# Matmuls of zeros on TensorE ahead of, and in the early pauses of, a fused attention and MoE kernel

## The chip, the cores and the metric

The kernel runs on one core of one Trainium2 chip. The metric is the device time in microseconds of one execution, and the number for a kernel is the median of its runs. The engines are PE (TensorE matmuls, with PEld for its weight loads), DVE (VectorE), ACT (ScalarE), POOL (GpSimd) and SP (SyncE, which issues the loads and stores).

## The reference

The input is q, k and v with 8 batches, 8 heads, 576 positions and 64 dimensions. For each batch and head there are two attentions, which are added; the sum goes through a two-layer network with a leaky ReLU.

```python
q_d = q.reshape(B, H, Sd, factor, D).mean(axis=3)      # factor 4, Sd 144; k_d and v_d likewise
out_d = sm_attn(q_d, k_d, v_d)                         # softmax attention over the 144 pooled positions
out_up = np.repeat(out_d, factor, axis=2)
mask = np.abs(pos[:, None] - pos[None, :]) < factor    # local attention: 7 neighbours
scores = np.where(mask, scale * np.matmul(q, k.transpose(0, 1, 3, 2)), -1000000000.0)
...
out_local = np.matmul(attn, v)
x = (out_up + out_local), transposed and reshaped to 4608 x 512
h = x @ w_in                                           # 512 x 2048
g = np.maximum(0.01 * h, h)
return g @ w_out                                       # 2048 x 512
```

## The kernel before

**The order of the work** is written by a planner at build time. Every piece of work is a Python generator that asks for slots (buffers) and for operations on an engine, and yields the estimated duration of each. The class `Order` keeps a time for each engine and always takes the operation that can start first; between equal ones the lower rank (the first argument of `od.spawn`) goes first. Instructions are emitted in the order in which the planner takes them, so each engine's queue has a fixed order, and on the chip an instruction that isn't ready holds up all that stand behind it on its engine. In the planner an operation is done `HOP` = 0.2 us after its end.

**The network.** Columns of x are handled in chunks: chunk 0 has 512 columns and chunks 1 to 11 hold the rest. `up_proj` (L843) multiplies by w_in into the bank `hp`; `leaky` (L854 to L857) makes the two halves `gh` and `gl` of the activations on ACT and DVE; `down_proj` (L881) multiplies by w_out into the banks `acc0` to `acc3`. Each product is three matmuls of high and low parts. The weights come in blocks, `convert` loads one (L245) and unpacks it on ACT (L313), DVE (L315), ACT or DVE again (L326, L323) and POOL (L328); the buffer is free for the next load after L328.

**The first batch's attention** is done ahead of that, with four pairs of heads c = 0 to 3, from buffers whose names begin with `su_`. Two kinds of work are interleaved:

- `pooled(0, c)`: sums of four positions (DVE L428 for c = 0, POOL L422 and L424 for the others), the scores into the bank `acc{c}` (PE L444), the softmax (DVE L452 and L453, ACT L456, DVE L459 and L460, POOL L464), two transposes (PE L477, copied out by ACT L479), the values (PE L501, copied out by ACT L507). `vsums` sums v on DVE (L391) as its loads land.
- `banded(0, c, hf)`: the local attention's scores in two parts hf (PE L556 and L564), the softmax (DVE L571 and L572, ACT L575, DVE L577, ACT L579, DVE L581, POOL L583), transposes (PE L591, copied out by ACT L593), the values (PE L606), the sum with the pooled part (DVE L617) and the split into x (ACT L629, DVE L631).

After that, POOL and DVE compute the local attention of the other seven batches (L691, L697, L752, L758) beside PE's network.

**What the change touches.** `heads` are two tiles of 128x512 int32 that DVE clears at the start (L284); `convert` writes the upper half of each of their elements at L313, from 23 us on. `slot("acc3")` is one bank of PSUM; its first use is the pooled scores of c = 3. The planner's time of an operation on PE starts at the later of the time of PE and of what it waits for.

Of the kernel before, what the change touches and what calls it, by code (L numbers as in the profile page):

```python
# [10 lines left out]
BF16 = mybir.dt.bfloat16  # L11
# [14 lines left out]
NF, NE, NC = DF // 128, DM // 128, DM // 128  # L26
# [11 lines left out]
LSPLIT = 14  # L38
HALFS = 4
HF1 = 21  # L40


def plan():
# [161 lines left out]
def attn_moe(ctx: ExitStack, tc, qkt, vd, qb, kb, vb, vwb, band, identb, w_in, w_out, ident, edge, out):  # L205
    nc = tc.nc
# [12 lines left out]
    od = Order(bufs)  # L219

    def slot(*tags):
        return (yield ("slot", tags, 0))
# [6 lines left out]
    def bank(s):  # L229
        return ps.tile([128, 512], F32, name=s.tag, tag=s.tag, bufs=bufs[s.tag])  # L230

    def op(eng, n, *after, times=1, lock=False):
        if eng == "PE":
            dur = n
        else:
            a, k = COST[eng]
            dur = times * a + k * n
        return (yield ("op", eng, dur, max((0.0,) + after), 0, after, lock))
# [9 lines left out]
    def wait(name, n=1):  # L248
        return (yield ("wait", name, n))
# [3 lines left out]
    def fixed():  # L253
        yield from wait(("asked", 0, 0))
        for dst, src, name, size in ((idb_sb, identb, "idb", 32e3), (band_sb, band, "band", 160e3),
                                     (id_sb, ident, "id", 64e3)):
            od.signal(name, (yield from load(dst, src, size)))

    def edges():
        yield from wait("late")  # L260
        od.signal("edge", (yield from load(edge_sb, edge, 32e3)))
# [20 lines left out]
    heads = [axp.tile([128, DM], I32, name=f"head{i}") for i in range(bufs["head"])]  # L282
# [5 lines left out]
    def cleared():  # L288
        yield from wait(("x", 0, 0), NC)
        for t in qblks:  # L290
            nc.gpsimd.memset(t[:, :384], 0)
            od.signal("cleared", (yield from op("POOL", 200, 0.0)))

    stage = []

    def staging():
        s_x = yield from slot("x1")
        stage.append(sb(s_x, [128, bufs["stage"], HALFS * DM], U16))
        od.signal("stage")
        s_x.free((yield from wait("converted", 2 * NF)))  # L300
# [36 lines left out]
    def outd_tile(b):  # L337
        s = yield from slot("outd")
        outd[b] = sb(s, [128, NC, SD], F32)
        od.signal(("outd", b), s.t)  # L340
        t = yield from wait(("read", b), 8 if b < BANDED else 2 * len(PARTS[b]))
        s.free(t)

    def x_tile(i):
        if i > 1:
            yield from wait(("xbuf", i - 1))
        elif i:
            yield from wait("stage")
        s_x = yield from slot(f"x{i % 2}")
        both = sb(s_x, [128, 2, NC, XMAX[i % 2]], F32R)[:, :, :, :CHUNKS[i][1]]  # L350
        xt[i] = both[:, 0], both[:, 1]
        od.signal(("xbuf", i), s_x.t)
        s_x.free((yield from wait(("done", i), 2 if i == 0 else 1)))
        if i >= LAST - 2:
            od.signal(("over", i))
# [14 lines left out]
    def given(c):  # L370
        if c:
            yield from wait(("asked", 0, c - 1))
        kept[0, c] = sup.tile([128, 2, S], F32, name=f"qk{c}")
        tq = yield from load(kept[0, c], qkt[0, c], 590e3)
        od.signal(("asked", 0, c))
        od.signal(("qk", 0, c), tq)
# [139 lines left out]
    def windows(c, hf, pool):  # L516
        b0, b1 = BLKS[hf]
        if hf:
            yield from wait(("vd", 0, c))
        s_vw = yield from slot("su_vs" if hf else "su_vw")  # L520
        vws[c, hf] = s_vw, sb(s_vw, [WIN, b1 - b0, 2, D], F32, pool)
        t = yield from load(vws[c, hf][1][:, :b1 - b0], vwb[0, c, :, b0:b1], 35840 * (b1 - b0), s_vw.t)
        od.signal(("vw", c, hf), t)
# [401 lines left out]
    def make_room():  # L925
        for c in range(NC):
            yield from wait(("pooled", B - 1, c))
        yield from wait("converted", 2 * NF)
        t = yield from wait("values", len(ORD))
        ax.__exit__(None, None, None)  # L930
        fin[1] = ctx.enter_context(tc.tile_pool(name="fin1", bufs=1))
        for h in range(2):
            raw[1, h] = unit(1, f"r1{h}", [128, 2, EN], F32)
        xt[LAST] = [unit(1, f"b{h}", [128, 2, EN], F32R) for h in "hl"]
        od.signal(("xbuf", LAST), t)
        t = yield from wait("landed", len(ORD))
        at.__exit__(None, None, None)
        fin[2] = ctx.enter_context(tc.tile_pool(name="fin2", bufs=1, side="right"))
        od.signal("cleared2", t)
# [11 lines left out]
    def combine_x():  # L951
        t = yield from wait(("xbuf", LAST))
        s_s = yield from slot("sw1")
        for h in range(2):
            raw[0, h] = unit(1, f"r0{h}", [128, 2, EN], F32)
        tx = yield from wait(("x", LAST - 1, 0), LANDED[LAST - 1, 0])
        xh, xl = (x.bitcast(F32) for x in xt[LAST - 1])
        for h in range(2):
            t = yield from op("POOL", 2 * EN, t, tx)
            both("POOL", raw[0, h], xh[:, 2 * h:2 * h + 2], xl[:, 2 * h:2 * h + 2], ALU.add)  # L960
        od.spawn(-3.5, split_x24())
        od.spawn(-3.4, split_x31())
        T["B22"] = xt[LAST][::-1]
        od.signal("B22", (yield from wait(("x", LAST, 0), LANDED[LAST, 0] // 2)))
        for j, h in (("B11", 0), ("B21", 1)):
            T[j] = [x[:, 2 * h:2 * h + 2] for x in xt[LAST - 1][::-1]]
            od.signal(j, tx)
        tr = yield from wait("raw", LANDED[LAST, 0])
        for o, a, b, alu in (((1, 0), (1, 1), (1, 0), ALU.subtract), ((0, 0), (0, 0), (1, 0), ALU.add),
                             ((0, 1), (0, 1), (0, 0), ALU.subtract), ((1, 1), (1, 1), (0, 0), ALU.subtract)):  # L970
            t = yield from op("DVE", 2 * EN, t, tr, lock=True)
            both("DVE", raw[o], raw[a], raw[b], alu)
            od.signal(("T", o), t)
        od.signal("Tdone", t)
        s_s.free((yield from wait("x24")))
# [147 lines left out]
    def split():  # L1123
        for f in range(NF):
            t = yield from wait(("kept", f))
            t = max(t, (yield from wait("turned")))
            s_g, s_l = (yield from slot("gh")), (yield from slot("gl"))
            od.spawn(-9 + 0.1 * f, halved(f, G[f // 2][:, f % 2], s_g, s_l, t))
# [24 lines left out]
    with tc.manual_schedule():  # L1153
        od.spawn(0, fixed())
        od.spawn(30, cleared())
        for b in range(B):
            od.spawn(0, outd_tile(b))
        od.spawn(0, staging())
        for i in range(LAST):
            od.spawn(0, x_tile(i))  # L1160
        od.spawn(0, make_room())
        od.spawn(-3, combine_x())
        for p in range(NP):
            od.spawn(-2 + 0.1 * p, combine_1(p))
        od.spawn(-9, split())
        od.spawn(5001, finale())
        for c in range(NC):
            od.spawn(0.1 * c + (0.1 if c else -1), given(c))
            od.spawn(1 + c, pooled(0, c, 1 + c, sup))
            od.spawn(1.1 + c, vsums(0, c, sup))  # L1170
            od.spawn(1.5 + c, banded(0, c, 0, 1.5 + c, sup))
            od.spawn(HF1 + 0.1 * c, banded(0, c, 1, HF1, sup))
            for hf in range(2):
                od.spawn(1.2 + c + 4 * hf, windows(c, hf, sup))
        for f in range(NF):
            for k in range(2):
                od.spawn(20 + 2 * f + k, convert(f, k))
        od.spawn(0, swap())
        od.spawn(0, edges())
        od.spawn(0, opened())  # L1180
        od.spawn(30, over())
        od.spawn(-1, outbuf())
        od.spawn(5000, down_proj())
        od.spawn(4999, up_proj())
        for b in range(BANDED, B):
            for c in range(NC):
                od.spawn(88 + 10 * b + 0.1 * c, pooled(b, c, 0))
                od.spawn(88 + 10 * b + 0.1 * c + 0.05, vsums(b, c))
            for i, j0, j1, c0 in PARTS[b]:
                for u in range(2):  # L1190
                    r = 10 * b + j0 + 0.5 * u
                    od.spawn(89 + r, scores(b, j0, j1, u))
                    od.spawn(90 + r, widen(i, b, j0, j1, u))
                    od.spawn(90 + r, values(i, b, j0, j1, c0, u))
        od.run()
# [62 lines left out]
```

## Time and profile before

| | |
|---|---|
| median of 3 runs | 937.95 us (935.0 to 939.55) |
| the profiled execution | 933.69 us |
| its span, first to last instruction | 931.9 us |
| mean granted clock of TensorE in it | 0.990 |
| bytes moved by DMA | 114.98 MB, a mean of 123 GB/s |

The profile comes from one execution. Busy time is given by engine, and "idle before" with the instruction or the transfer that ended the wait. The view of stretches gives each engine's busy time in a stretch, with the clock that TensorE was granted (1.00 is full speed) and the share of the time in which the DMA engines were busy. The timeline merges neighbouring instructions of one line: start, length, engine, line, operation, tiles, count, and in brackets the wait before it. The chain of waits follows the work that ended last back to the start.

### The profile page before, as it was taken

How to read it: one execution, taken by the hardware profiler on the slowest of the kernel's cores; microseconds unless marked ns; L12 is line 12 of the kernel's file. 1: busy time of each engine (PE TensorE's matmuls, PEld its weight loads, DVE VectorE, ACT ScalarE, POOL GpSimd, SP SyncE). 2: the span in 40 equal slices, each digit the busy share in tenths (PEclk: the TensorE clock that was granted, in tenths of full speed). 3: DMA queues.
4: the chain of work that ended last, by engine and by line, in shares of the span. 5: the costliest groups of instructions: out<-in, count | busy, mean ns of one | idle time of the engine just before them, and what ended most of it. 6: DMA issues, size and time to landing. Idle time of an engine off the chain costs nothing.

```text
span 931.9 us, 16300 instructions
## 1 busy us (share of the span) xinstructions
PE 907.9 (97%) x6066; PEld 888.0 (95%) x6066; DVE 625.5 (67%) x981; ACT 456.0 (49%) x1222; POOL 678.4 (73%) x408
## 2 busy tenths in 40 slices
PE   6898999999999999999999999999999999999997
PEld 4698999998999999999999999999999999999997
DVE  5899888988879886873754883862765865433322
ACT  4876754655646545553423553622522535544431
POOL 4677889899899996963984982894799886794100
PEclk7999999999999999999999999999999999999999
DMA  8886655655554552551431551342333310000000
GB/s 249 274 271 209 197 178 167 195 161 169 159 171 139 182 178 80 176 171 58 140 99 33 169 170 62 102 131 60 98 104 104 119 52 1 18 18 1 1 35 34
DMA packets 58784, 114.98 MB, mean 123 GB/s; under 512 B 6976, under 2 KB 23616, under 8 KB 58704
## 3 DMA queue, kind: packets, MB, share of 16 engines
q1 hardware_dynamic: 58704, 113.93, 40.1%
q8 instruction: 48, 0.79, 0.3%
q14 instruction: 32, 0.26, 0.1%
HBM read 104.47 MB, written 9.44 MB: 122 GB/s over the span
## 4 chain that ended last, share of the span: by engine, by line
PE 93%; DVE 2%; DMA 2%; ACT 1%; POOL 1%; issue 1%; SPq 0%; DVEq 0%; ACTq 0%; POOLq 0%
PE acc L881 39%; PE hp L843 35%; PE pt L1115 4%; PE pt L477 2%; PE pt L440 2%; PE pt L501 2%; PE hp L1115 2%; PE pt L881 2%; PE hp L881 2%; PE pt L790 1%; DMA prod<-in_w_in_dram 1%; DMA qk<-in_qkt_dram 1%; DMA out_dram<-olot 0%; POOL prod L752 0%; ACT head L313 0%
## 5 line engine op out<-in xcount | busy, mean ns | idle before, releaser
L843 PE MATMUL hp<-x,wi 128*128 128x384 f32 (+1 forms) x2112 | 378.4, 326 | 7.1 <-DVE gl L857 7.1
L843 PEld LDWEIGHTS hp<-x,wi 128*128 128x128 f32 x2112 | 340.9, 191 | 9.7 <-DVE gl L857 7.9
L691 POOL TENSOR_TENSOR prod<-q,k 128x1344 f32<-128x1344 f32 x84 | 260.0, 3095 | 75.9 <-DVE xloc L758 58.0
L752 POOL TENSOR_TENSOR prod<-v,s 128x1344 f32<-128x1344 f32 x84 | 262.1, 3123 | 3.4 <-DVE xloc L758 1.4
L881 PE MATMUL acc<-gh,woh 128*128 128x384 f32 (+1 forms) x768 | 250.5, 326 | 0.3 <-ACT olot L912 0.3
L881 PE MATMUL acc<-gh,wol 128*128 128x384 f32 (+1 forms) x768 | 246.9, 321 | 0.0
L881 PE MATMUL acc<-gl,woh 128*128 128x384 f32 (+1 forms) x768 | 246.8, 321 | 0.0
L857 DVE TENSOR_TENSOR gl<-hp,gh 128x384 fp32r<-128x384 f32 (+1 forms) x184 | 95.4, 520 | 147.0 <-ACT hp L855 144.7
L854 ACT ACTIVATE gh<-hp 128x384 fp32r<-128x384 f32 (+1 forms) x184 | 85.9, 467 | 201.2 <-PE acc L881 192.6
L881 PEld LDWEIGHTS acc<-gh,woh 128*128 128x128 f32 x768 | 144.9, 189 | 1.4 <-ACT olot L912 0.6
L881 PEld LDWEIGHTS acc<-gl,woh 128*128 128x128 f32 x768 | 145.0, 189 | 0.0
L881 PEld LDWEIGHTS acc<-gh,wol 128*128 128x128 f32 x768 | 144.8, 189 | 0.0
L697 DVE TENSOR_REDUCE s<-prod 128x21 f32<-128x1344 f32 x84 | 129.4, 1540 | 5.9 <-POOL prod L691 5.8
L758 DVE TENSOR_REDUCE xloc<-prod 128x192 f32<-128x1344 f32 x76 | 117.2, 1542 | 4.6 <-POOL prod L752 4.6
L855 ACT ACTIVATE hp<-hp 128x384 f32<-128x384 f32 (+1 forms) x184 | 84.6, 460 | 0.0
L456 ACT ACTIVATE pd<-pt,st_d 128x144 f32<-128x144 f32 x84 | 32.1, 382 | 48.2 <-DVE st_d L453 37.7
L796 DVE TENSOR_TENSOR pt<-pt,up 128x384 f32<-128x384 f32 x42 | 37.7, 897 | 23.0 <-PE pt L790 20.0
L777 ACT COPY up<-outd 128x576 f32<-128x576 f32 x84 | 52.3, 675 | 0.1
L479 ACT COPY ptd<-pt 72x288 f32<-72x288 f32 x64 | 25.1, 398 | 33.8 <-PE pt L477 33.5
L391 DVE TENSOR_REDUCE v_d<-vs 72x128 f32<-72x512 f32 x56 | 37.5, 669 | 1.3 <-DMA vs<-in_vd_dram 1.0
L811 ACT CAST x<-pt 128x384 fp32r<-128x384 f32 x38 | 18.5, 488 | 32.9 <-DVE pt L796 32.8
L468 ACT ACTIVATE pd<-pd,st_d 128x144 f32<-128x144 f32 x84 | 28.7, 411 | 0.9 <-DVE st_d L460 0.9
(189 smaller groups left out, 1075.6 us busy)
## 6 DMA issues: line engine op xcount, KB each, us to landing
k<-in_kb_dram SPq DMA_DIRECT2D x84, 288.0 KB
v<-in_vb_dram SPq DMA_DIRECT2D x84, 288.0 KB
qk<-in_qkt_dram SPq DMA_DIRECT2D x32, 576.0 KB
vs<-in_vd_dram SPq DMA_DIRECT2D x56, 144.0 KB
q<-in_qb_dram SPq DMA_DIRECT2D x84, 96.0 KB
out_dram<-olot SPq DMA_DIRECT2D x40, 192.0 KB
x<-in_w_in_dram SPq DMA_DIRECT2D x10, 511.8 KB
x<-in_w_out_dram SPq DMA_DIRECT2D x7, 511.8 KB
```

What stands on the lines that cost most here:

```text
L691: nc.gpsimd.tensor_tensor(out=prv, in0=q[:, a - j0:z - j0].unsqueeze(2).to_broadcast([128, n, W, D]), in1=view(k, (a - j0) * D, [[D, n], [ ...
L697: nc.vector.tensor_reduce(out=s[:, p, a - j0:z - j0], in_=prv, axis=AX.X, op=ALU.add)
L752: nc.gpsimd.tensor_tensor(out=prv, in0=view(v, 0, [[1, nj], [nv, D], [1, W]]), in1=s[:, p, :nj].unsqueeze(2).to_broadcast([128, nj, D, W]) ...
L758: nc.vector.tensor_reduce(out=xl_t[:, :nj, p], in_=prv, axis=AX.X, op=ALU.add)
L777: nc.scalar.copy(out=up[:, pp], in_=outd[b][:, 2 * u + pp].unsqueeze(2).to_broadcast([128, SD, FAC]))
L796: nc.vector.tensor_tensor(out=xv, in0=xv, in1=upv, op=ALU.add)
L843: nc.tensor.matmul(hp[:, :n], w[h][:, ws], x[:, c], start=c + j == 0, stop=c == NC - 1 and j == 2)
L854: nc.scalar.activation(out=gh[:, :n], in_=hp[:, :n], func=AF.Prelu, alpha=0.01)
L855: nc.scalar.activation(out=hp[:, :n], in_=hp[:, :n], func=AF.Prelu, alpha=0.01)
L857: nc.vector.tensor_tensor(out=gl[:, :n], in0=hp[:, :n], in1=gh[:, :n].bitcast(F32), op=ALU.subtract)
L881: nc.tensor.matmul(acc[:, a:z], w[h][:, es], g[:, :n], start=(a, f, j) == (0, 0, 0), stop=f == NF - 1 and j == 2, skip_group_check=ch == 0)
L1115: nc.tensor.matmul(held[b][1][:, :EN], w[h][:, c * 128:(c + 1) * 128], T[x][m][:, c], start=c + j == 0 and name not in BEFORE, stop=c == 1 ...
```

## The change

One constant and one generator are added, and the generator is spawned with rank 9000, behind all others. It takes the bank acc3, multiplies 128 columns of a tile of zeros by 512 columns of the same tile (read as bf16) nine times, each planned at 0.43 us one after the other, and from 7.0 to 16.0 us of the planner's time it puts one more, planned at 0.22 us, wherever PE has nothing that could start as early. Then it gives the bank back. Nothing reads the result.

```diff
+WARM = 16.0
...
+    def busy():
+        s_b = yield from slot(f"acc{NC - 1}")
+        pad, idle = bank(s_b), heads[-1].bitcast(BF16)
+        t = 0.0
+        for i in range(9):
+            t = yield from op("PE", 0.43, t, s_b.t)
+            nc.tensor.matmul(pad, idle[:, :128], idle[:, 128:640], start=True, stop=True)
+        t = max(t, 7.0)
+        while t < WARM:
+            t = yield from op("PE", 0.22, t + 0.05)
+            nc.tensor.matmul(pad, idle[:, :128], idle[:, 128:640], start=True, stop=True)
+        s_b.free(t)
...
+        od.spawn(9000, busy())
```

## The prediction

> **What bounds the kernel now.** I read the page first: span and engine shares.
>
> ```profile
> span 931.9 us, 16300 instructions
> PE 907.9 (97%) x6066; PEld 888.0 (95%) x6066; DVE 625.5 (67%) x981; ACT 456.0 (49%) x1222; POOL 678.4 (73%) x408
> ```
>
> PE is the bound over the whole: 931.9 - 907.9 leaves 24.0 us in which it did nothing. The change touches only its first 16 us or so, so the second view is the stretches of 2 us there (after the stretch and its length: busy time and count of PE, PEld, DVE, ACT, POOL, then granted clock, DMA share, GB/s).
>
> ```profile
> 10.00:12.00 2.00, 0.86 (x12) 0.59 (x12) 1.47 (x7) 1.03 (x5) 2.00 (x3) 1.00 0.85 156
> 12.00:14.00 2.00, 1.47 (x6) 0.65 (x6) 0.41 (x2) 1.40 (x7) 1.80 (x3) 0.55 0.79 170
> 20.00:22.00 2.00, 2.00 (x15) 1.42 (x15) 0.77 (x3) 1.18 (x6) 0.73 (x1) 0.50 0.98 299
> 22.00:24.00 2.00, 2.00 (x35) 1.60 (x33) 1.16 (x4) 1.50 (x4) 0.18 (x1) 0.89 1.06 249
> 28.00:30.00 2.00, 1.13 (x7) 0.63 (x7) 1.67 (x4) 2.00 (x6) 2.00 (x3) 1.00 1.01 265
> ```
>
> The granted clock falls to half shortly after 12 us, behind a stretch in which PE was busy for 0.86 of 2 us, and comes back soon after 22 us. In that slow stretch PE is full (2.00 of 2.00) and the other engines are not: there PE sets the pace. The PE timeline says which work is slow.
>
> ```profile
> 5.09 0.39 PE L556 MATMUL hp<-band_sb,idb_sb 128*128 128x280 bf16 x1 [5.09 <-DMA band_sb<-in_band_dram]
> 6.39 1.65 PE L444 MATMUL acc<-qk_d 64*64 64x144 f32 x12
> ...
> 9.91 0.95 PE L444 MATMUL acc<-qk_d 64*64 64x144 f32 x12 [0.69 <-POOL qk_d L424]
> 12.01 0.72 PE L477 MATMUL pt<-id_sb,v 128*72 128x128 f32 x3 [1.14 <-POOL v L464]
> ...
> 14.31 0.85 PE L477 MATMUL pt<-id_sb,v 128*72 128x128 f32 x3 [0.84 <-ACT ptd L479]
> ...
> 15.31 1.71 PE L444 MATMUL acc<-qk_d 64*64 64x144 f32 x12
> 16.94 1.23 PE L501 MATMUL pt<-ptd,su_vd 72*64 72x144 f32 x8
> ...
> 18.89 1.12 PE L606 MATMUL acc<-su_pt,su_vw 70*64 70x64 f32 x16
> ...
> 21.61 1.08 PE L564 MATMUL hp<-qk 64*64 64x67 f32 x16
> 22.52 0.90 PE L444 MATMUL acc<-qk_d 64*64 64x144 f32 x12
> 23.35 0.72 PE L501 MATMUL pt<-ptd,su_vd 72*64 72x144 f32 x8
> 24.00 0.30 PE L591 MATMUL pt<-id_sb,xloc 128*70 128x128 f32 x1
> 24.55 0.49 PE L477 MATMUL pt<-id_sb,v 128*72 128x128 f32 x3 [0.25 <-ACT outd L507]
> 24.97 0.69 PE L606 MATMUL acc<-su_pt,su_vw 70*64 70x64 f32 x16
> ...
> 26.16 0.70 PE L564 MATMUL hp<-qk 64*64 64x67 f32 x16
> ```
>
> The same twelve matmuls of L444 take 1.65, 0.95, 1.71 and 0.90 us. So PE is slow twice: in its first work (the clock column shows 1.00 there, but 1.65 us is the slow duration) and from about 12.4 to 22.3 us. Between 14.31 and 23 us PE waits for nothing.
>
> **The change part by part.** *Nine matmuls ahead of the first work.* They read a tile that DVE clears at the very start:
>
> ```profile
> 0.91 1.03 DVE L284 MEMSET head<- 128x512 int32 x2 [0.91 <-PEq L1241]
> 885.20 8.32 PE acc L881 x48
> ```
>
> So they start near 2.0 us. No row has a 128x512 bf16 matmul. The last row is from the chain of waits: 48 matmuls over 384 columns in 8.32 us, 0.173 us each at full clock. By columns 512 take 0.23 us, and 0.46 us at half clock (an estimate; the bounds are 0.173 and twice 0.23). Nine slow ones end at 2.0 + 9 x 0.46 = 6.1 us, 1.0 us past the 5.09 at which the first real matmul starts now. If the clock is up by then, L564 and L444 take about 0.4 and 0.7 us less, and L444 ends near 7.9 instead of 8.04; if not, about 0.9 us later than now. What hides this is POOL and the loads in front of the next step:
>
> ```profile
> 9.94 1.15 POOL L422 TENSOR_TENSOR su_half<-qk 128x576 f32<-128x576 f32 x1
> ...
> 10.62 0.18 DVE L460 RECIPROCAL st_d<-st_d 128x3 f32<-128x3 f32 x1
> ...
> 11.04 0.91 POOL L464 TENSOR_TENSOR v<-v,st_d 128x432 f32<-128x432 f32 x1
> ```
>
> L464, which the L477 of 12.01 waits for, stands behind L422 on POOL, which ends at 11.09; its own input from DVE's L460 was ready at 10.80, 0.24 us before it starts. Without that cover the whole 0.9 counts; with it 0.9 - 0.24. Cost at 12 us: 0 to +0.7; I take 0, because the clock came up some 3.5 us after PE's first work now (between the L444 of 6.39 and that of 9.91), and 2.0 + 3.5 = 5.5 is before the first real matmul.
>
> *Matmuls in the pauses up to 16 us of the plan.* The plan puts one at most every 0.22 + 0.20 + 0.05 = 0.47 us where PE has nothing planned, so at most 9 / 0.47 = 19; with the real work of that stretch taken out, about 14. A real matmul that becomes ready behind one waits for the rest of it: 0.23 us at most at full clock, and the pauses in the rows (0.69, 1.14, 0.84 us) hold most of them. Two stand in the full stretch ahead of the L444 of 15.31: +0.46.
>
> *The clock stays up from 12 to 22 us.* Slow against fast durations of the same lines: L477 0.85 to 0.49 (0.36, three times on this path), L591 likewise (0.36, once), L444 1.71 to 0.95 (0.76), L501 1.23 to 0.72 (0.51), L606 1.12 to 0.69 (0.43), L564 1.08 to 0.70 (0.38). Sum 1.08 + 0.36 + 0.76 + 0.51 + 0.43 + 0.38 = 3.5 us, less the 0.46: PE comes 3.0 us sooner to the end of the L591 of 24.00, at 21.3.
>
> *What is late next.* These rows of the other engines decide it:
>
> ```profile
> 18.69 1.22 DVE L391 TENSOR_REDUCE su_vd<-su_vs 72x256 f32<-72x1024 f32 x1 [0.33 <-DMA su_vs<-in_vd_dram]
> ...
> 23.02 0.76 ACT L313 CAST head<-prod 128x512 f16<-128x512 bf16 x1 [0.50 <-DMA prod<-in_w_in_dram]
> ...
> 23.77 0.44 ACT L575 ACTIVATE xloc<-xloc 128x280 f32<-128x280 f32 x1
> ...
> 24.12 0.28 ACT L507 COPY outd<-pt 128x144 f32<-128x144 f32 x1
> ...
> 24.77 0.44 DVE L577 TENSOR_REDUCE lst<-xloc 128x4 f32<-128x280 f32 x1
> ...
> 26.25 0.68 DVE L315 SCALAR_TENSOR_TENSOR prod<-prod,head 128x512 int32<-128x512 int32 x1
> ```
>
> ACT comes to L313 and waits 0.50 us for the first weight block. The loads ahead of it have kept the DMA share near 1.0, and PE's clock doesn't hasten them. Behind L313 in ACT's queue stand L575 and L507; PE's next L477 waits for that L507. So of 3.0 us on PE, ACT lets through nothing at 23.77. DVE's L577 needs L575, over at 24.21, and starts at 24.77 only because DVE had PE's late results to work off: 24.77 - 24.21 = 0.56 us can go, and L315, which starts the weight pipeline, moves by that. One more wait for a load follows:
>
> ```profile
> 30.81 8.84 DMA prod<-in_w_in_dram
> 39.73 0.78 ACT head L313
> ```
>
> This load is issued when L328 frees its buffer, up to 0.56 us sooner now; it shares a nearly full wire, so it lands 0 to 0.56 us sooner. I take **-0.4 us**, nearer the issue than the wire, as the chain of waits goes through the issue.
>
> *At nothing:* the bank (acc3), which is next written by the L444 of 22.52 on the same engine in queue order; the zeros tile, next written by a later L313, long after; DVE, ACT, POOL and SP get no instruction.
>
> Sum: the profiled execution took 933.69 us (span 931.9, 1.8 around it), 4.3 below the median 937.95. It becomes 933.3, and the median 937.95 - 0.4 = **937.5**.
>
> **Rivals.** *A, the clock drops later instead (slower).* If PE is done with L591 at 21.3 and L507 still comes at 24.12, PE pauses for 3 us where it paused for 0.25. Pauses of that kind do cost the clock here:
>
> ```profile
> 78.00:79.00 1.00, 0.20 (x2) 0.00 (x0) 1.00 (x2) 0.70 (x3) 1.00 (x2) 1.00 0.12 45
> ```
>
> ```profile
> 80.00:90.00 10.00, 9.31 (x66) 9.31 (x67) 9.22 (x13) 4.74 (x11) 7.79 (x5) 0.83 0.55 188
> ```
>
> After a pause of over 1.8 us from 78 us on, the next 10 us have a granted clock of 0.83: 1.7 us of PE's clock are gone, or 3.4 us at half speed. Against it: 28 to 30 us with PE busy for 1.13 of 2 us keeps 1.00. Price: L477 twice, L606, L564 and L501 slow, 0.72 + 0.43 + 0.38 + 0.51 = 2.0 us, in work that DVE and ACT wait for; less the 0.4; 939.5. It decides where the pause fills more than about half of the stretch by which the chip judges.
> The Trainium skill, "TensorE: Matmul & The Clock Gate", section "Why this matters for your kernels", says that gaps above about 3 us drop the clock; by that A hangs on a tenth of a microsecond. The trace disagrees: pauses of 0.69 and 1.14 us were enough before 12 us. The same page of the Trainium skill, section "What's actually happening", says that the window of about 3.4 us runs freely, so A could come in some executions and not in others; one trace can't show that.
>
> *B, PE's whole gain reaches the end:* -3.0, 935.0. For it, PE is the bound over 97%; against it, the wait of L313, and DVE's waits for loads (L391 at 18.69). It needs another order on ACT.
>
> *C, the zeros don't lift the clock* (the change doesn't do what it says): 14 at 0.46 is 6.4 us, less the pauses of 2.7: +3.7, 941.6. Against it, nothing in the trace shows that the operands' values matter.
>
> *D, another order further on.* The planner books the extra matmuls, so real ones are planned up to 0.2 us later, and its choices for DVE, ACT and POOL may tip anywhere in 930 us. One pause of PE more or less like
>
> ```profile
> PE hp L843 <- DVE gl L857: 7.1, 4, 2.5
> ```
>
> (four, the longest 2.5 us) with the 1.7 us of clock lost behind the one near 80 us, is 2.5 + 1.7 = 4.2 us: 942.1 or 933.7.
>
> **How the numbers follow.** Forecast 0.38, A 0.27, B 0.10, C 0.06, D 0.19 (half each way). About 0.5% (4.7 us: below 933.3, above 942.6) is what a measurement of this kernel can tell from no change. Only D, or a case with the spread of the three times before (935.0 to 939.55) on top, gets past that: faster 0.11, slower 0.10, same 0.79. The range takes in A, B and C and most of D: 933.0 to 942.0.
>
> **What would show it.** Right: the first PE work is at 2.0 us in zeros; the L444 near 15.3 takes about 0.95 us; the granted clock is 1.00 from 12 to 20 us; L313 still starts near 23.0 with a longer wait (about 2 us) before it; the pause before L477 grows to 3 us; from 40 us on everything is where it was within 0.5 us. A shows as a clock of 0.50 between 24 and 30 us and slow L606 and L564 there; C as 0.50 throughout 12 to 22; D as other counts of pauses L843 <- DVE gl and another order of lines. The forecast is wrong if L313 starts well before 22.5 us.

## The result and the profile after

The changed kernel takes 939.77 us, the median of 18 runs (936.73 to 942.13). The kernel before, run beside it, takes 933.46 us (18 runs, 931.51 to 939.55). The ratio is **1.0062**, with a 95% interval of 1.0049 to 1.0074: slower by about 0.6%, or 5.8 us (the two medians themselves lie 6.3 us apart). The median of 937.95 us from which the prediction started came from three runs, and lay 4.5 us above that of the eighteen.

First the page of the changed kernel: its span, engine rows, and the slices of granted clock.

```profile
span 937.7 us, 16327 instructions
...
PE 914.5 (98%) x6089; PEld 889.6 (95%) x6089; DVE 633.1 (68%) x981; ACT 456.5 (49%) x1222; POOL 678.2 (72%) x408
...
PEclk9699999999999999999999999999999999999999
```

The span is 5.8 us longer. The second slice of the clock, from 23.4 to 46.9 us, is the odd one. Here is PE's timeline of the changed kernel. The matmuls of zeros are L301 and L305. The inserted lines move the numbers behind them by 14: L327 was L313, L458 was L444, L491 was L477, L515 was L501, L521 was L507, L570 was L556, L578 was L564, L589 was L575, L605 was L591, L620 was L606.

```profile
2.00 4.02 PE L301 MATMUL acc<-head 128*128 128x512 bf16 x9 [2.00 <-DVE head L285]
5.81 0.39 PE L570 MATMUL hp<-band_sb,idb_sb 128*128 128x280 bf16 x1
...
8.58 1.04 PE L305 MATMUL acc<-head 128*128 128x512 bf16 x4
...
14.92 0.95 PE L458 MATMUL acc<-qk_d 64*64 64x144 f32 x12
...
16.91 0.69 PE L620 MATMUL acc<-su_pt,su_vw 70*64 70x64 f32 x16
...
20.44 0.30 PE L605 MATMUL pt<-id_sb,xloc 128*70 128x128 f32 x1
26.09 0.82 PE L491 MATMUL pt<-id_sb,v 128*72 128x128 f32 x3 [5.35 <-ACT outd L521]
26.84 1.12 PE L620 MATMUL acc<-su_pt,su_vw 70*64 70x64 f32 x16
```

The matmuls of zeros do what they are there for: the L458 of 14.92 takes 0.95 us instead of 1.71, and PE is through with its L605 at 20.74 instead of 24.30. Then it waits for **5.35 us** for one copy on ACT, and the L620 behind that is slow again: 1.12 against the 0.69 of 16.91. Stretches of 2 us show the clock (columns as in the prediction):

```profile
20.00:22.00 2.00, 0.74 (x9) 0.35 (x5) 1.61 (x5) 0.00 (x0) 0.89 (x1) 1.00 1.00 320
22.00:24.00 2.00, 0.00 (x0) 0.00 (x0) 0.00 (x0) 0.98 (x2) 0.00 (x0) 0.77 1.04 304
24.00:26.00 2.00, 0.00 (x0) 0.00 (x0) 1.57 (x2) 1.03 (x5) 0.00 (x0) 0.50 1.03 253
...
28.00:30.00 2.00, 2.00 (x20) 1.53 (x20) 1.16 (x5) 0.37 (x1) 0.91 (x1) 0.50 1.01 285
...
34.00:36.00 2.00, 2.00 (x23) 1.44 (x23) 1.54 (x4) 1.06 (x2) 2.00 (x2) 0.50 0.78 233
36.00:40.00 4.00, 3.52 (x20) 2.71 (x20) 3.50 (x6) 3.06 (x8) 2.64 (x3) 0.50 0.73 204
40.00:44.00 4.00, 4.00 (x57) 3.57 (x56) 3.65 (x5) 2.84 (x7) 3.04 (x4) 0.98 0.73 237
```

The slow stretch of 10 us has moved from 12 to 22 us to 23 to 40 us, and there it is 17 us long. From 22 to 40 us the kernel before had a mean clock of 0.99, and the changed one has 0.53:

```profile
22.00:40.00 18.00, 15.37 (x202) 11.57 (x200) 15.63 (x34) 13.79 (x39) 11.81 (x11) 0.99 1.00 285
```

```profile
22.00:40.00 18.00, 13.13 (x110) 9.76 (x111) 11.21 (x23) 11.23 (x32) 7.99 (x7) 0.53 0.88 261
```

Why ACT is late stands in the timeline of the changed kernel:

```profile
23.02 0.76 ACT L327 CAST head<-prod 128x512 f16<-128x512 bf16 x1 [3.08 <-DMA prod<-in_w_in_dram]
23.65 0.42 ACT L589 ACTIVATE xloc<-xloc 128x280 f32<-128x280 f32 x1
...
25.05 0.76 ACT L327 CAST head<-prod 128x512 f16<-128x512 bf16 x1 [0.97 <-DMA prod<-in_w_out_dram]
25.68 0.27 ACT L521 COPY outd<-pt 128x144 f32<-128x144 f32 x1
```

ACT waits for the first weight block until 23.02, the very time of before. But then comes the unpack of the **second** block, which lands at 25.05, and only behind that L521, the copy that PE waits for. In the kernel before, that unpack stood further down:

```profile
28.13 0.77 ACT L313 CAST head<-prod 128x512 f16<-128x512 bf16 x1
```

So the change has altered the order on ACT. In the planner's own times, the second unpack can start at 22.43 us, when its block has landed, and an instruction of a clearly lower rank that is ready within 0.4 us of that goes first (`AHEAD`). L507 was ready at 22.71, 0.28 us later. With the matmuls of zeros booked on PE it is ready at 22.84, 0.41 us later, and is passed over by 0.01 us. From there on the queues differ: PE's plan does at some 520 of its 1836 positions. If the planner is kept from this one choice, every queue has the order of before again, so no other choice tipped by itself.

### The profile page after: what moved, and what is told of

Same layout as the page of the kernel before. It is cut to its first block, busy times and chain, and to the rows that moved or that the text cites. A ratio compares the mean times of both kernels' runs of the same rounds, so it can differ in the third digit from the quotient of the medians.

```text
span 937.7 us, 16327 instructions
## 1 busy us (share of the span) xinstructions
PE 914.5 (98%) x6089; PEld 889.6 (95%) x6089; DVE 633.1 (68%) x981; ACT 456.5 (49%) x1222; POOL 678.2 (72%) x408
## 4 chain that ended last, share of the span: by engine, by line
PE 91%; DVE 4%; DMA 3%; issue 1%; ACT 1%; DVEq 0%; ACTq 0%
PE acc L895 38%; PE hp L857 35%; PE pt L1129 4%; PE pt L491 2%; PE pt L454 2%; PE pt L515 2%; PE hp L1129 2%; PE pt L895 2%; PE hp L895 2%; PE pt L804 1%; DMA prod<-in_w_out_dram 1%; DVE x L329 1%; DMA su_vw<-in_vwb_dram 1%; DVE woh L337 1%; ACT head L327 0%
## 5 line engine op out<-in xcount | busy, mean ns | idle before, releaser
L857 PE MATMUL hp<-x,wi 128*128 128x384 f32 (+1 forms) x2112 | 377.0, 326 | 4.5 <-DVE gl L871 3.2
L857 PEld LDWEIGHTS hp<-x,wi 128*128 128x128 f32 x2112 | 339.8, 190 | 8.4 <-DVE gl L871 4.6
```

What stands on the lines that cost most here:

```text
L857: nc.tensor.matmul(hp[:, :n], w[h][:, ws], x[:, c], start=c + j == 0, stop=c == NC - 1 and j == 2)
```

## Experiments

The theories: (1) the exchange on ACT lengthens the pause, and the clock that lapses in it costs the time; (2) the new order costs it anywhere in 930 us, whatever the clock does; (3) the matmuls of zeros themselves cost it. Every kernel was timed beside the kernel before, and all ratios are to that. The changed kernel itself was not timed beside these runs, so differences from it are differences of two ratios. Clocks and stretches come from one profiled execution of each.

**The order alone (e1).** The planner books the operations, and no matmul is issued.

```diff
         for i in range(9):
             t = yield from op("PE", 0.43, t, s_b.t)
-            nc.tensor.matmul(pad, idle[:, :128], idle[:, 128:640], start=True, stop=True)
...
             t = yield from op("PE", 0.22, t + 0.05)
-            nc.tensor.matmul(pad, idle[:, :128], idle[:, 128:640], start=True, stop=True)
```

> The changed kernel without its matmuls of zeros: the planner still books them, so every queue has the changed order, and the chip runs none. Theory 1 (the clock lapses in the longer pause, and that costs the time): the clock is slow from 12 to 22 us as before the change, PE comes late to the pause, the pause is 1 to 2 us and the clock holds; about 1.5 us over the kernel before, from the second unpack of a weight block that now stands ahead of L521 on ACT. Theory 2 (the new order costs the time by itself, anywhere in 930 us): all of the 6 us over the kernel before. Theory 3 (the pads themselves cost it): no difference from the kernel before.

Measured: 1.0083 (1.0068 to 1.0098), no faster than with the matmuls. So theory 3 falls; theory 2's expectation, all of the 6 us, comes nearest, and theory 1 fails in its expectation for this run. That rested on PE being slow from 12 to 22 us without the zeros; the profile shows that this isn't always so (its L455 is L444, its L488 is L477, its L518 is L507):

```profile
14.35 0.52 PE L488 MATMUL pt<-id_sb,v 128*72 128x128 f32 x3 [1.34 <-ACT ptd L490]
...
14.96 0.95 PE L455 MATMUL acc<-qk_d 64*64 64x144 f32 x12
...
27.12 0.83 PE L488 MATMUL pt<-id_sb,v 128*72 128x128 f32 x3 [5.71 <-ACT outd L518]
```

In this execution the clock stayed up through the early pauses with no zeros at all, and lapsed in the long pause just the same (0.54 over 22 to 40 us).

**The matmuls alone (e2).** The same 23 matmuls at the same places of PE's queue, in the order of before: the planner emits them ahead of certain of PE's operations (`PADS`: the bank, then the operation's number and how many) and books nothing.

```diff
+PADS = (("acc3", {0: 9, 2: 1, 3: 4, 4: 4, 5: 2, 6: 1, 7: 2}),)
...
+                if eng == "PE" and task[0] != 9000:
+                    self.extra(self.pe)
+                    self.pe += 1
```

> The kernel before with the same 23 matmuls of zeros at the same places of PE's queue, put in without booking them, so that the order of all else is that of before. Theory 1: ACT now reaches its first weight unpack with L507 behind it about 2 us early and waits for the load; PE pauses for about 3 us near 21 to 24 us; if the clock lapses there the time is 1 to 3 us over the kernel before, if it holds it is 0.5 us under. Theory 2: no slower than before, 0 to 1 us under. Theory 3: all of the 6 us over.

Measured: 1.0013 (0.9997 to 1.0029), between the two branches of theory 1 and not told from no change. Its profile shows the forecast's picture, the wait of L477 (here L498) for L507 (here L528) among it:

```profile
PE pt L498 <- ACT outd L528: 3.3, 1, 3.3
```

and a clock of 0.72 over 22 to 40 us:

```profile
22.00:40.00 18.00, 15.83 (x163) 11.88 (x164) 14.04 (x30) 13.37 (x37) 9.37 (x9) 0.72 1.00 291
```

**A first try at holding the clock (e3)**, with 25 more matmuls in the pause of the changed kernel, by the same means.

```diff
+PADS = (("acc2", {18: 25}),)
```

> The changed kernel with 25 more matmuls of zeros (5.4 us at full clock) in the pause of 5.35 us, into the bank acc2, which is free then; not booked, so the order is that of the changed kernel. Theory 1: the clock stays at 1.00 through 20 to 40 us, PE does its work of 26 to 40 us at full speed, and 3 to 5 us of the 6 come back. Theory 2: the order keeps the time where the changed kernel has it, within 1 us.

Measured: 1.0112 (1.0095 to 1.0129), slower still, but the run didn't do what was meant. The zeros are the tile that ACT's second unpack writes, so these matmuls (L325) waited for ACT's unpack (L348) too, and filled PE after the pause instead of in it:

```profile
PE acc L325 <- ACT head L348: 4.9, 1, 4.9
```

It says nothing on the clock. It does show that PE is on the path there: 25 matmuls put between the pause and PE's work cost some 4.7 us over the changed kernel (0.0050 of 935).

**The order of before, with the pause filled (e4).** As the matmuls alone, and 13 in the pause.

```diff
+PADS = (("acc3", {0: 9, 2: 1, 3: 4, 4: 4, 5: 2, 6: 1, 7: 2}), ("acc2", {18: 13}))
```

> The kernel before, its own order, with the 23 matmuls of zeros and 13 more (2.8 us) ahead of the L477 that waits for ACT's L507. Theory 1: the clock holds from 5 us to the end of the setup, and what is left of the gain is what ACT's wait for the first weight block lets through: 0.5 us under the kernel before, at most 3. Theory 3: slower than the run without the 13.

Measured: 1.0002 (0.9984 to 1.0019). The clock didn't hold to the end of the setup: it fell at about 31 us, in the smaller pauses there (0.76 over 22 to 40 us). The time is not told apart from that of e2.

**One exchange on ACT in the kernel before (e6)**, and nothing else: the second unpack is emitted ahead of L507 and all other orders are kept.

```diff
+SWAP = 18
...
+        def unpack():
+            nc.scalar.copy(out=head.bitcast(F16).rearrange("p (m h) -> p m h", h=2)[:, :, 1], in_=top)
...
+        if (f, k) == (0, 1):
+            od.swap = unpack
         t = yield from op("ACT", 600, t, s_u.t)
-        nc.scalar.copy(out=head.bitcast(F16).rearrange("p (m h) -> p m h", h=2)[:, :, 1], in_=top)
+        if (f, k) != (0, 1):
+            unpack()
```

> The kernel before, no matmuls of zeros, with one pair of instructions exchanged on ACT: the unpack of the second weight block (L313, first block of w_out) stands ahead of L507, the copy that PE's L477 waits for; all other queues and the rest of ACT's are those of before. Theory 1 (the one exchange, by its pause and the clock that lapses in it): 4 to 8 us over the kernel before. Theory 2 (the later order that the planner builds on the exchange costs the time): at most 2 us over.

Measured: 1.0023 (1.0002 to 1.0043), 2.1 us, below what theory 1 said and at the edge of theory 2. Its executions lie far apart, and the clock with them: the shortest, of 931.27 us, had a mean granted clock of 1.000, the two longest, of 940.37 and 941.3 us, 0.979. That fits a price of the exchange that is mostly clock, but one execution at 1.000 doesn't show it.

**The exchange undone in the changed kernel (e7)**, with its zeros and its later order: the unpack is emitted right behind L521.

```diff
+SWAP = 19
...
         t = yield from op("ACT", 600, t, s_u.t)
+        if (f, k) == (0, 1):
+            od.swap = unpack
+        else:
+            unpack()
```

> The changed kernel with its matmuls of zeros and with the order of the changed kernel everywhere but for this one pair on ACT: L521 stands ahead of the unpack of the second weight block again. Theory 1: the pause shrinks to about 3 us and the time comes within 2 us of the kernel before. Theory 2: it stays 4 to 6 us over the kernel before.

Measured: 1.0041 (1.0023 to 1.0059), 3.8 us over the kernel before: 2.0 us less than the changed kernel, though the two intervals overlap, and nearer to what theory 2 said than to theory 1. The pause is 2.5 us instead of 5.35 (L502 is L477, L532 is L507), but the clock still lapses in it:

```profile
PE pt L502 <- ACT outd L532: 2.5, 1, 2.5
```

```profile
22.00:40.00 18.00, 14.95 (x133) 11.51 (x135) 13.09 (x26) 12.72 (x35) 9.40 (x9) 0.62 0.93 293
```

**The clock held in the changed kernel (e8).** 25 matmuls of 512 columns in the pause, from two constants that nothing writes; all queues but PE's are as in the changed kernel.

```diff
+PADS = (("acc2", {18: 25}),)
...
+        idle = band_sb.rearrange("p a k -> p (a k)")
...
+                    nc.tensor.matmul(pads[tag], idb_sb, idle[:, :512], start=True, stop=True)
```

> The changed kernel with 25 more bf16 matmuls of 512 columns in its pause, from two constant tiles that nothing writes then (the run with pads from the zeros tile had to wait for the unpack, which writes that tile). Theory 1a (the lapse of the clock in the pause is what costs): the clock holds through 20 to 40 us and 3 to 5 of the 6 us come back. Theory 1b (the pause itself and the late weight pipeline cost it, and PE's speed after it doesn't matter): within 1 us of the changed kernel.

Measured: 1.0021 (1.0005 to 1.0038). This is theory 1a: the step from 1.0062 is 0.0041, **3.8 us** (about 2 to 6), and the two intervals don't meet. The pause is as long as before, only filled, and everything behind it is fast (L325 is the 25 matmuls, L512 is L477, L641 is L606):

```profile
20.59 5.56 PE L325 MATMUL acc<-band_sb,idb_sb 128*128 128x512 bf16 x25
26.00 0.49 PE L512 MATMUL pt<-id_sb,v 128*72 128x128 f32 x3
26.42 0.69 PE L641 MATMUL acc<-su_pt,su_vw 70*64 70x64 f32 x16
```

```profile
22.00:40.00 18.00, 16.17 (x186) 11.10 (x184) 14.76 (x30) 13.49 (x38) 11.04 (x9) 1.00 0.97 287
```

ACT and DVE gain with PE, as they work off what PE hands them: 13.49 and 14.76 us busy from 22 to 40 us, against 11.23 and 11.21 in the changed kernel.

**Both at once (e11)**: the exchange undone, and 13 matmuls in the pause that is left.

```diff
+SWAP = 19
+PADS = (("acc2", {18: 13}),)
```

> The changed kernel with the pair on ACT put back (as e7) and 13 matmuls in the pause that is left (as e8), so neither the long pause nor the lapse is there and only the order after 24 us is that of the changed kernel. If that order has no price of its own: 0 to 2 us under the kernel before. If it has one: 1 to 3 us over, near the run e8.

Measured: 1.0011 (0.9994 to 1.0028), and in its profile a clock of 0.91 from 22 to 40 us. So the changed kernel's later order and its zeros, taken together, are not told from no change. Against the same zeros in the order of before with the clock held (e10 below, timed beside it) it is 0.22 points slower, with the two intervals overlapping: a price of the later order alone is neither shown nor excluded.

**The true landing times in the plan (e9)**: the first two weight blocks are planned 2.6 us later.

```diff
+LATE = 2.6
...
+        if f == 0:
+            t += LATE
         t = yield from op("ACT", 600, t, s_u.t)
```

> The changed kernel with 2.6 us added to the planner's time at which the first two weight blocks have landed (the chip shows 23.0 and 25.05 us; the planner has them some 2.5 us earlier). The unpacks then stand behind the attention's copies on ACT and the pause goes. If the pause and the lapse are what counts: 1 to 3 us under the kernel before. If any other order has its own price: anywhere within 8 us of it.

Measured: 1.0017 (0.9999 to 1.0034). The clock is 1.00 from 12 to 40 us, so the lapse is gone with no matmuls in the pause. But nothing is won over the kernel before, where the first branch of the expectation had 1 to 3 us. This order has another pause: PE's longest wait for DVE (L860 is L843, L874 is L857) is 4.2 us, near 72 to 76 us, against 2.5 in the kernel before, and the mean clock from 60 to 80 us is 0.91.

```profile
PE hp L860 <- DVE gl L874: 7.5, 3, 4.2
```

**The order of before, held longer (e10)**: as the run with the 13, and 14 more in the smaller pauses between 27 and 33 us.

```diff
+PADS = (("acc3", {0: 9, 2: 1, 3: 4, 4: 4, 5: 2, 6: 1, 7: 2}), ("acc2", {18: 13}), ("acc0", {23: 3, 24: 4, 26: 3, 28: 2, 29: 2}))
```

> The kernel before in its own order with matmuls of zeros up to 16 us, 13 in the pause near 21 to 24 us (as the run e4), and 14 more of bf16 constants in the smaller pauses between 27 and 33 us, where the clock fell in e4. If the clock holds to 40 us and PE's speed there counts: 2 to 4 us under the kernel before. If the weight pipeline sets the time from 40 us on: within 1 us of the kernel before.

Measured: 0.9989 (0.997 to 1.0007), with a clock of 1.00 from 12 to 60 us. So even with PE at full clock through the whole setup, the kernel is not measurably faster than before: with zeros in this order the gain is at most 0.3%.

Where the time is lost and found again is seen in the network's matmuls (`hp`, `acc` and the last chunks' products) that have started by a given time, counted in one stretch from 0 us on in the views of these three lines:

| started by | before | changed | clock held (e8) | exchange undone and held (e11) | zeros in the old order (e2) |
|---|---|---|---|---|---|
| 40 us | 24 | 4 | 20 | 15 | 20 |
| 60 us | 120 | 94 | 122 | 106 | 120 |
| 120 us | 522 | 439 | 467 | 453 | 522 |
| 300 us | 1552 | 1526 | 1547 | 1533 | 1561 |
| 900 us | 4791 | 4757 | 4785 | 4770 | 4800 |

At 900 us the changed kernel is 34 matmuls behind; at the 0.173 us apiece of the prediction's row that is 5.9 us, its whole loss. It is behind by 20 at 40 us and by 83 at 120 us, and by 26 at 300 us: it catches up, since its PE is hardly ever idle from 120 to 300 us. The stretch in the kernel before, then in the changed one:

```profile
120.00:300.00 180.00, 176.66 (x1315) 173.24 (x1314) 156.79 (x258) 102.00 (x322) 162.51 (x89) 0.99 0.55 169
```

```profile
120.00:300.00 180.00, 179.94 (x1368) 176.83 (x1368) 160.58 (x260) 105.25 (x327) 163.63 (x90) 1.00 0.55 166
```

With the clock held the start is nearly that of before, and only 6 are missing at 900 us. At 120 us it is 55 behind all the same, as e11 is by 69: that much comes with the later order, and most of it is made up by 300 us. These are single executions; that of e8 took 934.83 us, 1.6 less than its median.

Over a whole execution the change costs no clock: the mean granted clock is 0.989 in the changed kernel (18 executions) and 0.989 in the kernel before (79, beside the experiments). In the profiles it moves the slow stretch, from ahead of the first weight block, where ACT waits for a load in any case and holding the clock gained nothing that was measured, to behind it, where holding it gives 3.8 us back.

## Why the prediction was wrong

It said -0.4 us and a range up to 942.0; measured were +5.8 us and 939.77 us. The time lies in the range only because the median that it was added to was 4.5 us too high; the sign and the chances (0.10 for slower by over 0.5%) were wrong.

- *The nine matmuls, and those in the pauses*: right. They start at 2.00, the first real matmul comes at 5.81 instead of the estimated 6.1, four in a row take 1.04 us, and 12 us is reached without a delay (L491 at 11.54 against 12.01).
- *The clock from 12 to 22 us*: right in the profiles compared. PE came to the end of L605 at 20.74, the text said 21.3. But e1's clock held there without zeros, so this gain isn't there in every execution.
- *What is late next*: half right. ACT waits for the first weight block until 23.02, as said. **The step that failed is "Behind L313 in ACT's queue stand L575 and L507"**: it took ACT's order for that of before. In the changed kernel the second unpack stands there too, so the pause ends at 26.09 instead of about 24.4, the end of L507 in the kernel before, and lasts 5.35 us instead of 3. With the old order (e2) the pause is 3.3 us, as rival A said, and the time is within the noise of no change, as forecast.
- *The -0.4 us itself* can be read in e2, which keeps the order. DVE's L315 starts at 25.08 instead of 26.25, 1.17 us sooner where the text had 0.56. But the load that ends ACT's wait near 39.7 lets L313 start at 39.61 instead of 39.73, 0.12 us sooner. In these two executions the term was too large, and no time here can tell it from nothing.
- *Rival D* held the very mechanism, the planner's bookings that tip a choice, but put it "anywhere in 930 us" and half each way. It struck one choice only, at the place where ACT waits for a load, where another instruction in front can only lengthen the wait.
- *Rival A* was the right mechanism, mis-sized, and made an alternative to D where D set it off. Its price was one series of slow matmuls, 2.0 us. The clock stayed down for 17 us, and holding it gives 3.8 us back.

The sum as the runs have it: 0.62% in all; 0.41 points (about 0.2 to 0.6) are the lapse of the clock behind the pause (changed kernel against e8). The remaining 0.21 (0.05 to 0.38) is what the longer pause and the later order cost, less what the zeros gain. Undoing the exchange as well brings it to 0.11 (-0.06 to 0.28), so its split stays open. Open too is whether and why the order alone (1.0083, from four executions) is slower than the changed kernel (1.0062), as their intervals overlap: the zeros' gain before 20 us may be the reason, but e1's profile, fast there without them, doesn't show it.

## What to carry to other kernels

Work that is planned moves other work, even where it is meant to fill idle time: compare the queues of both kernels around the first place where an engine waits for a load, before any sum is made. The same matmuls put in without a booking (e2) left the order alone and cost nothing that was measured. An instruction that waits for a transfer should not stand ahead of a copy that the bounding engine needs. A faster engine comes sooner to the next wait, and where the clock follows its activity, the pause there takes back what the speed has won.

## What the runs showed of the hardware

Four things were not expected.

**The clock came back only 17 us after it fell.** In the changed kernel it fell some 2.3 us after the pause's start (the mean of 0.77 from 22 to 24 us puts it at 23.1) and stayed at 0.50 until 40 us, though PE was full for most of 28 to 40 us (2.00 of 2.00). The work there is many small matmuls of 64 to 72 rows or columns and transposes. By contrast the kernel before lost 1.7 us of clock behind its pause near 80 us, 3.4 us at half speed, where the work is the network's dense matmuls. The Trainium skill, "TensorE: Matmul & The Clock Gate", section "What's actually happening", has only the first 3.4 us or so of a busy stretch at the slow clock and everything after at the full one; the stretch near 80 us agrees, that of 28 to 40 us does not. The same page of the Trainium skill, section "Part 4: PE-mode transpose", says that transposes don't count as busy in the same way, which would fit; no run here took the transposes alone. What ends a slow stretch stays open: in the kernel before the clock came back near 22.4 us among small matmuls of the same lines (L564, L444).

**The same pauses don't always cost the clock.** Before L477 the kernel before paused for 1.14 us and was slow from 12.2 us on; the order-only run (e1) paused for 1.14 us at the same place, then for 1.34 us before the next L477, and stayed fast:

```profile
11.87 0.52 PE L488 MATMUL pt<-id_sb,v 128*72 128x128 f32 x3 [1.14 <-POOL v L475]
```

**Matmuls of zeros lift the clock like any others**: nine of them, from 2.0 to 6.0 us, and the first real matmuls of L578 behind them ran at full speed.

```profile
6.13 0.70 PE L578 MATMUL hp<-qk 64*64 64x67 f32 x16
```

**The clock differs between executions of one kernel, and the time with it.** Of the 18 executions of the changed kernel, the five with a mean granted clock of 0.985 or 0.986 took 940.02 to 940.88 us, and the three at 0.995 took 936.73 to 939.18 us; the clock isn't all of it, as the longest, of 942.13 us, had 0.991. In e10 the four at 1.000 took 930.4 to 932.43 us, the two at 0.992 936.9 and 936.93 us.
